# A fused attention and expert kernel: scale sizes, row gathers and weight measures put at other steps

## The chip, the cores and the metric

The kernel runs on one core of one Trainium2 chip. The metric is the device time of one execution in microseconds (us). Before the change it was 986.37 us, the median of three runs (983.27 to 987.94).

## The reference, cut to what matters

Eight batches of eight heads with 576 tokens of 64 features go through attention in which only scores within `tau` of the row's maximum count. The output is laid out as 4608 rows of 512 features. Each row then goes to one of eight experts:

```python
scores = scale * np.matmul(q, k.transpose(0, 1, 3, 2))
thresh = np.max(scores, axis=-1, keepdims=True) - tau
scores = np.where(scores >= thresh, scores, -1e9)
attn = softmax(scores)                       # with 1e-9 in the divisor
x = np.matmul(attn, v)                       # -> 4608 rows of 512
e_idx = np.argmax(x @ w_gate, axis=1)
out[mask_e] = gate_w * sigmoid(x @ w_output_gate)[e] * (relu(x @ w1[e]) @ w2[e])
```

The weights `w1[e]` are 512 x 1024 and `w2[e]` 1024 x 512, all in float32.

## The kernel before, in words

**Attention** (`Attention.run`, line 342) is a loop over columns `g`. Nine columns (`T`) are a step `m`, which takes two units (a unit is one head of a pair of batches), and there are 16 steps, so 144 columns (`G`, `end`), and six more that drain the pipeline. A column computes a tile of scores on PE (line 145), copies and reduces it on VectorE (159), takes exponentials on ScalarE (177) and masks on VectorE (189), transposes, and multiplies by v. The threshold between comes from GpSimd (166). The order in PE, VectorE, ScalarE and GpSimd is that of the program, written out by hand; SP's order, which issues the direct loads, is left to the framework's planner. Work from elsewhere is hung on columns by a table `hooks`, run at the column's end.

**Routing** (`Router`). After every fourth step a batch pair's rows are scattered by GpSimd (line 547) to `xs` in DRAM, grouped by expert. Rows of the first three pairs (group "A") fill the early units; the rest is spread over ten slots of fixed sizes, `SLOTS`. `choose` (679) picks greedily for each slot in turn which expert it serves; it is a generator, first one step and then three steps per slot (the third writes `picks`, line 701), and `aside` (497) runs some of its steps per column. `finish` (709) scatters rows of zeros behind the last row of each expert, the eight *pads*, and makes the remaining tables.

**Experts.** There are thirteen units: three early ones (366, 256 and 424 rows, units 0 to 2) and one per slot, in the order `UNITS` (780). `Experts.run` (1038) gives each unit eight columns `f`, each 128 of the 1024 hidden features: `first` (1178) multiplies rows by w1 (line 1187, 12 matmuls), ScalarE does the relu (1189), ScalarE and VectorE split the result into a high half `hh` and a low half `hl` (940, 946), and one column later `second` (1193) multiplies by w2 (1207 to 1209). Precision is kept by splitting each float32 operand in two float16 halves, after scaling by powers of two. So for the weights:

- `load_next` (1010) loads a chunk (a quarter of an expert, 1 MB in two DMAs, line 831) when a buffer is free and its slot is picked. There are four buffers for even and four for odd units.
- `look` (984) measures a chunk's largest value three columns later (`measure`, 855: VectorE line 858 and ScalarE line 859). In column 0 it measures whatever of the next unit is left, and `top` (866) reduces the eight numbers per row (869, 870: `red`), transposes them on PE (871) and takes the maximum. In column 3 `spread` (881) spreads it to all rows.
- `split_until` (1022) splits the chunks into halves (942 on ScalarE, 948 on VectorE).

And for the rows: `gather` loads them from `xs` into the one buffer `xg`, `even` (896) takes each row's largest value on VectorE (899, `ax`) and scales the row on ScalarE (906), `prep` transposes in two columns (1163, or 1279 for units whose size isn't whole tiles) and splits. Before the change the gather of unit i+1 is issued in column 0 of unit i (column 1 if that is unit 2), `even` in column 4 (5) and `prep` in columns 5 and 6 (6 and 7). `Pair.load` (1247) makes a slot's gather wait for all row scatters and all pads.

**During attention** the twelve chunks of the early units are loaded (`glance`) and measured (`size`) from hooks, one per nine columns, and after the last columns unit 0 is prepared by hooks.

Of the kernel before, what the change touches and what calls it, by code (L numbers as in the profile page):

```python
# [17 lines left out]
P = 128  # L18
# [412 lines left out]
class Router:  # L431
# [4 lines left out]
    def __init__(self, ctx, tc, ntok, E, DM, sizes, cut):  # L436
# [55 lines left out]
        self.odd = ctx.enter_context(tc.tile_pool(name="rodd", bufs=1))  # L492
        self.ripe, self.side, self.last = False, [], False
        self.xrows, self.queue, self.pending, self.placed, self.tables = {}, [], None, None, []
        self.gate, self.kind = None, None

    def aside(self, n):
        for _ in range(n):
# [210 lines left out]
    def finish(self):  # L709
        nc, E, sm, row, dummy = self.nc, self.E, self.sm, self.row, self.dummy  # L710
        V = nc.vector
        pad = sm.tile([P, E], F32, name="padf")
        padi = sm.tile([P, E], I32, name="padi")
        held = sm.tile([P, E], F32, name="held")
        V.tensor_scalar(pad, self.cnt, self.pid, None, op0=ALU.add)
        V.tensor_tensor(held, pad, self.first, op=ALU.subtract)
        V.tensor_scalar(held, held, float(self.SAFE), float(1 << 20), op0=ALU.is_lt, op1=ALU.mult)
        V.tensor_tensor(padi, pad, held, op=ALU.add)
        yield "vector"
        self.pads = []  # L720
        for e in range(E):
            self.pads.append(self.scatter(self.zrow, padi[:, e : e + 1], "pad"))
            if e % 2:
                yield "vector"
        while not self.chosen:
            yield "vector"
        ni, nf, v, ci, st = row(E, "ni", I32), row(E, "nf"), row(E, "v"), row(E + 1, "ci"), self.st
        V.tensor_scalar(nf, st[:, 0], float(P - 1), 0.0, op0=ALU.add, op1=ALU.max)
        V.tensor_copy(ni, nf)
        V.tensor_scalar(ni, ni, 7, None, op0=ALU.arith_shift_right)  # L730
        V.tensor_copy(nf, ni)
        V.tensor_scalar(v, st[:, 2], -1.0, dummy, op0=ALU.mult, op1=ALU.add)
        yield "vector"
        yield from self.sums(ci, nf)
        V.tensor_copy(self.total, ci[:, E : E + 1])
        yield from self.table(sm, "s", self.rows, ci, P, v)
        self.tables.append("s")
# [39 lines left out]

class Experts:
    RB, NW, YB = 4, 4, 4
    UNITS = (2, 6, 0, 7, 3, 8, 1, 5, 9, 4)  # L780
    TURN = (2,)
    LOOK, MEASURE = 3, 3

# [79 lines left out]
        V.tensor_scalar(up.bitcast(I32), src.bitcast(I32), EXPONENT, EXPONENT, op0=ALU.bitwise_and, op1=ALU.bitwise_xor)  # L863
        V.tensor_scalar(down.bitcast(I32), src.bitcast(I32), EXPONENT, None, op0=ALU.bitwise_and)

    def top(self, mx, ps):
        nc, V, n = self.nc, self.nc.vector, mx.shape[1]
        red = self.kp.tile([P, 8], F32, name="red")[:, 0:n]
        V.tensor_reduce(red, mx, axis=AX.X, op=ALU.max)
        V.tensor_scalar(red, red, UP, FLOOR, op0=ALU.mult, op1=ALU.max)  # L870
        nc.tensor.transpose(ps[0:n, 0:P], red, self.ident)

        def out():
            g = self.kp.tile([8, 1], F32, name="most")[0:n]
            self.diag = self.kp.tile([8, 8], BF16, name="diag")[0:n, 0:n]
            V.tensor_reduce(g, ps[0:n, 0:P], axis=AX.X, op=ALU.max)
            V.tensor_scalar(self.diag, self.ident[0:n, 0:n], g, None, op0=ALU.mult)

        return out
# [96 lines left out]
    def size(self, j):  # L976
# [3 lines left out]
        if e == 0:  # L980
            self.raws.append(raw)
            self.nload += 1

    def look(self, i, f, final):
        if self.fresh and self.column - self.fresh[0][2] >= self.LOOK:
            n, raw, _ = self.fresh.pop(0)
            if n % 4 == 0:
                self.mx[n // 4] = self.kp.tile([P, 2, 4], F32, name="mx")
            self.measure(raw, self.mx[n // 4], n % 4)
        n = i + 1  # L990
        if n < self.rt.early or final:
            return
        tile = lambda: self.ps_x.tile([P, 512], F32, name="px")
        if f == 0:
            while any(x[0] // 4 == n for x in self.fresh):
                k, raw, _ = self.fresh.pop(0)
                if k % 4 == 0:
                    self.mx[k // 4] = self.kp.tile([P, 2, 4], F32, name="mx")
                self.measure(raw, self.mx[k // 4], k % 4)
            self.top(self.mx.pop(n), tile())()  # L1000
        if f == 3:
            self.spread([n], tile())()

    def unit(self, i):
# [33 lines left out]
    def run(self):  # L1038
        rt, nun = self.rt, len(self.make)
        rt.open(self.ctx)  # L1040
        self.split_until(4)
        prev, fin = None, False
        for i in range(nun):
            b, final = self.unit(i), i == nun - 1
            late = i == rt.early - 1
            for f in range(8):
# [13 lines left out]
                    prev = (b, f)  # L1060
                self.look(i, f, final)
                k = f - (6 if late else 5)
                if not final and k == -1:
                    self.unit(i + 1).even()
                if not final and k in (0, 1):
                    self.unit(i + 1).prep(k)
# [4 lines left out]
                    rt.place(self.ps_x.tile([P, 512], F32, name="px")[:, 0:144])()  # L1071
                for _ in range(6 if rt.last else 3 if i or f else 0):
                    rt.advance(most=1)
                rt.aside(1 if rt.tables and i < rt.early else 2 if i else 4)
                if late and f == 1:
                    self.unit(i + 1).gather()
                self.split_until(2 * self.used + (4 if f % 2 else 3) - (i == 0))
                if final and f == 4:
                    self.tc.keep_in_program_order(self.nc.gpsimd.drain())
                if not (final or late) and f == 0:  # L1080
                    self.unit(i + 1).gather()
                self.load_next()
                self.column += 1
                if not rt.queue and not fin:
# [151 lines left out]
class Pair(Base):  # L1236
# [10 lines left out]
    def load(self, dst, r0, n):  # L1247
        rt = self.ex.rt
        src = rt.xs[bass.ds(self.row + r0, n), :]
        ins = self.nc.sync.dma_start(dst, src if n < P else src.rearrange("(t p) w -> p t w", p=P))  # L1250
        rt.after(ins, [x for _, x in rt.tok])
        rt.after(ins, rt.pads)

    def gather(self):
        self.xg = self.ex.gp.tile([P, 4, self.ex.rt.W], F32, name="xg")
# [149 lines left out]
def build(tc, qkv, tau, wg, w1, w2, out, shape):  # L1405
    nc = tc.nc
    with ExitStack() as ctx:
# [6 lines left out]
        with tc.manual_schedule(engines=ENGINES):  # L1414
            with ExitStack() as actx:
# [3 lines left out]
                end = at.G  # L1419
                ws = []  # L1420
                hooks[1] = lambda: ex.begin()
                W = 9
                for j in range(4 * rt.early):
                    g = end - 7 - W * (4 * rt.early - 1 - j)
                    hooks[g - 16] = lambda j=j: ex.glance(j)
                    hooks[g] = lambda j=j: ex.size(j)
                early = list(range(rt.early))
                hooks[end - 5] = lambda: at.jobs.append(lambda ps: ex.top(ex.early, ps))
                hooks[end - 3] = lambda: at.jobs.append(lambda ps: ex.spread(early, ps))
                hooks[end - 6] = lambda: ex.unit(0).gather()  # L1430
                hooks[end - 2] = lambda: outs.append(ex.unit(0).even(False))
                hooks[end - 1] = lambda: (ws.extend(ex.first_chunk()), outs.pop(0)())
                outs = []

                def prep(k):
                    pt = at.ps_s.tile([P, 1024], F32, name="ps")
                    ex.px = lambda: [pt[:, 0:512], pt[:, 512:]]
                    ex.unit(0).prep(k, outs)

                def second():  # L1440
                    prep(1)
                    outs[0]()
                    ws[0]()
                    ws[1]()

                def third():
                    outs[1]()
# [6 lines left out]
                    ws[2]()  # L1454
                    ws[3]()

                hooks[end] = lambda: prep(0)
                hooks[end + 1] = second
                hooks[end + 2] = third
                hooks[end + 4] = first  # L1460
                at.run(hooks)
            ex.open()
# [51 lines left out]
```

## Time and profile before

| | us |
|---|---|
| median of three runs | 986.37 |
| lowest and highest | 983.27, 987.94 |
| the profiled execution's own time | 986.73 |
| its span, first to last instruction | 985.0 |
| busy: PE, VectorE (DVE), ScalarE (ACT), GpSimd (POOL) | 899.8, 779.7, 734.0, 385.7 |

Times in the profile are us from the start of the span; `L871` is line 871 of the kernel before. Engines work side by side, so busy times don't add up to the span, and a matmul's end is modelled, so a busy PE isn't PE at its peak. What ends a wait is named behind an arrow. The granted clock is the share of TensorE's full clock of 2.4 GHz.

### The profile page before, as it was taken

To read this page: it belongs to the slowest core of one execution; us is meant where nothing else is said; L and a number is where in the kernel's file an instruction comes from. 1 tells how busy PE (TensorE), PEld (TensorE's weight loads), DVE (VectorE), ACT (ScalarE), POOL (GpSimd) and SP (SyncE) were. 2 spreads that over 40 slices of the span, in tenths; PEclk is the share of its full clock that TensorE was granted. 3 is DMA by queue.
4 is the path that set the end of the run, shared out by engine and by line. 5 is a ranking of instruction groups with operands and counts; after the bars stand their busy time and mean duration, and the time that the engine had idled before them with its cause. 6 is when DMAs were issued, how large, how long until landed. Compare 5 with 4: busy or idle time off the path is not lost. (4 is left out here: it accounts for less than half of the span.)

```text
span 985.0 us, 22613 instructions
## 1 busy us (share of the span) xinstructions
PE 899.8 (91%) x8367; PEld 544.0 (55%) x8367; DVE 779.7 (79%) x1889; ACT 734.0 (75%) x1406; POOL 385.7 (39%) x660
## 2 busy tenths in 40 slices
PE   8999999999999999999994596898898898898996
PEld 4666666665666666665553353445455345455543
DVE  7999999999999899999683756687677567668741
ACT  6999999998999989988762736567568567668642
POOL 4465657668666586776365000201002001002011
PEclk9999999999999999999898788899999999999999
DMA  4469633334433343331394605536545436544001
GB/s 158 144 220 293 179 122 98 107 110 138 133 121 109 118 152 96 111 115 55 114 325 158 201 22 178 200 99 201 171 150 163 150 109 190 171 150 141 22 21 43
DMA packets 77009, 136.92 MB, mean 139 GB/s; under 512 B 6792, under 2 KB 37768, under 8 KB 76897
## 3 DMA queue, kind: packets, MB, share of 16 engines
q1 hardware_dynamic: 70353, 115.29, 37.0%
q0 software_dynamic: 6544, 20.16, 5.4%
q8 instruction: 67, 1.10, 0.5%
q14 instruction: 45, 0.37, 0.1%
HBM read 103.65 MB, written 32.74 MB: 138 GB/s over the span
## 5 line engine op out<-in xcount | busy, mean ns | idle before, releaser
L177 ACT ACTIVATE p<-s,mn 128x576 f32<-128x576 f32 x288 | 215.3, 794 | 28.8 <-DVE s L159 28.6
L189 DVE SCALAR_TENSOR_TENSOR p<-s,thr,p 128x576 f32<-128x576 f32 x288 | 226.2, 822 | 5.0 <-POOL thr L166 4.4
L159 DVE TENSOR_SCALAR_CACHE_REDUCE s<-ps 128x576 f32<-128x576 f32 x288 | 206.2, 751 | 15.7 <-PE ps L145 13.9
L930 POOL DMA_INDIRECT out_dram<-yo,kid x39 | 46.3, 1186 | 382.6 <-DVE yo L929 244.6
L145 PE MATMUL ps<-qk 64*128 64x288 f32 (+1 forms) x1280 | 186.5, 419 | 0.7 <-DVE s L159 0.4
L166 POOL TENSOR_SCALAR thr<-mn,tau_sb 128x2 f32<-128x2 f32 x144 | 103.4, 718 | 134.2 <-DVE s L159 131.1
L1187 PE MATMUL ph<-xh,w1h 128*128 128x256 f16 (+7 forms) x412 | 135.9, 331 | 0.0
L1187 PE MATMUL ph<-xh,w1l 128*128 128x256 f16 (+7 forms) x412 | 134.8, 329 | 0.7 <-DVE w1l L948 0.7
L1187 PE MATMUL ph<-xl,w1h 128*128 128x256 f16 (+7 forms) x412 | 133.8, 329 | 0.0
L1189 ACT ACTIVATE hr<-ph 128x256 f32<-128x256 f32 (+7 forms) x103 | 48.0, 466 | 113.2 <-PE ph L1187 111.9
L145 PEld LDWEIGHTS ps<-qk 64*128 64x128 f32 (+1 forms) x1280 | 109.4, 177 | 21.8 <-DVE s L159 6.4
L946 DVE TENSOR_TENSOR hl<-hr,hh 128x256 f16<-128x256 f32 (+7 forms) x103 | 54.4, 528 | 78.3 <-ACT hh L940 75.4
L1187 PEld LDWEIGHTS <-w1h 128*128 128x128 f16 x832 | 81.8, 101 | 52.4 <-issue 6.2
L258 PE MATMUL pr<-PTb,vld 128*64 128x320 f32 (+1 forms) x640 | 107.1, 447 | 0.0
L244 PE MATMUL pt<-ident,p 64*128 64x64 f32 x2288 | 96.2, 224 | 1.5 <-ACT PTb L250 1.2
L244 PEld LDWEIGHTS pt<-ident,p 64*128 64x128 f32 x2288 | 83.4, 140 | 2.6 <-ACT PTb L250 1.5
L258 PE MATMUL pa<-PTa,vld 128*64 128x256 f32 (+1 forms) x640 | 84.7, 392 | 0.0
L1207 PE MATMUL py<-w2h,hh 128*128 128x512 f16 (+3 forms) x213 | 82.8, 389 | 0.0
L1208 PE MATMUL py<-w2l,hh 128*128 128x512 f16 (+3 forms) x213 | 82.7, 388 | 0.0
L1209 PE MATMUL py<-w2h,hl 128*128 128x512 f16 (+3 forms) x213 | 82.1, 385 | 0.5 <-DVE hl L946 0.2
L948 DVE SCALAR_TENSOR_TENSOR w1l<-r,up,w1h 128x1024 f16<-128x1024 f32 x40 | 51.2, 1280 | 30.0 <-ACT w1h L942 29.0
L324 POOL TENSOR_TENSOR rows<-xl,rinv 128x256 f32<-128x256 f32 x64 | 62.1, 970 | 14.6 <-ACT xl L369 14.3
(237 smaller groups left out, 1756.1 us busy)
## 6 DMA issues: line engine op xcount, KB each, us to landing
r<-in_moe_w_dram SPq DMA_DIRECT2D x120, 512.0 KB
qk<-in_qkv_dram SPq DMA_DIRECT2D x31, 608.0 KB
xs<-zrow SPq DMA_DIRECT2D x44, 257.0 KB
vld<-in_qkv_dram SPq DMA_DIRECT2D x32, 320.0 KB
xg<-xs SPq DMA_DIRECT2D x4, 771.0 KB
xg<-xs SPq DMA_DIRECT2D x6, 514.0 KB
xg<-xs SPq DMA_DIRECT2D x3, 1028.0 KB
xg<-xs SPq DMA_DIRECT2D x6, 128.5 KB
```

Source lines behind the costliest of these rows:

```text
L145: nc.tensor.matmul(ps[a][rows, o : o + HS], q[pp, t * P : t * P + w], k[pp, k0 : k0 + HS], start=True, stop=True)
L159: nc.vector.tensor_scalar(s, ps[a][:, c0 : c0 + S], SC, None, op0=ALU.mult, op1=ALU.min, accum_out=mn[:, a : a + 1])
L166: self.router.gate = nc.gpsimd.tensor_scalar(thr, mn, self.tau, None, op0=ALU.add)
L177: self.nc.scalar.activation(e, ss[a], AF.Exp, bias=mn[:, a : a + 1], scale=-1.0)
L189: nc.vector.scalar_tensor_tensor(e, s, thr[:, a : a + 1], e, op0=ALU.is_le, op1=ALU.mult, accum_out=acc[:, a ^ (t > 1) : (a ^ (t > 1)) + 1])
L244: nc.tensor.transpose(pt[:, o : o + 64], p[hs[h], k0 : k0 + P], id_[hs[h], hs[h]])
L258: one = lambda out, l, r, start, stop: nc.tensor.matmul(out, l, r, start=start, stop=stop, skip_group_check=True)
L324: nc.gpsimd.tensor_tensor(o, xl[:, a, 0:4, 0:D], ra[:, a, 0:4, None].broadcast_to([P, 4, D]), op=ALU.mult)
L1187: nc.tensor.matmul(ph, w[:, c, fs], x[:, c, 0:N], start=(i == 0), stop=(i == 11))
L1207: nc.tensor.matmul(Y, hh[:, ts], wh, start=(f == 0), stop=False)
L1208: nc.tensor.matmul(Y, hh[:, ts], wl, start=False, stop=False)
L1209: nc.tensor.matmul(Y, hl[:, ts], wh, start=False, stop=(f == 7))
```

## The change

- **Measures in other steps of attention.** The twelve chunks are measured in steps 2, 3, 4, 6, 7, 8, 10 to 15 (third column), instead of steps 4 to 15, and loaded in a list of columns instead of sixteen columns ahead.
- **Unit 0's start.** Its gather moves from column `end - 6` to `end - 2`, its pass over the rows from `end - 2` to `end`, behind the first weight half; transposes, key and second half follow one column later each.
- **Sizes.** `top` is cut in two: `peak` makes `red` in column 0, the transposition comes in column 3 and `spread` in column 4.
- **Rows.** `even` comes in column 3 (4 in unit 2). The gather of unit i+2 comes in column 7 of unit i, if it is an early unit or a picked slot with all pads issued; unit 3 keeps its place in unit 2.
- **Unit 3** takes slot 0 (420 rows) and unit 5 slot 2 (512 rows). A gather from slot 0 doesn't wait for the pads.
- **Picking.** Two steps per column in unit 2, where it was one.

```diff
-        self.gate, self.kind = None, None
+        self.gate, self.kind, self.pads = None, None, []
...
-    UNITS = (2, 6, 0, 7, 3, 8, 1, 5, 9, 4)
+    UNITS = (0, 6, 2, 7, 3, 8, 1, 5, 9, 4)
...
-    def top(self, mx, ps):
-        nc, V, n = self.nc, self.nc.vector, mx.shape[1]
+    def peak(self, mx):
+        V, n = self.nc.vector, mx.shape[1]
         red = self.kp.tile([P, 8], F32, name="red")[:, 0:n]
         V.tensor_reduce(red, mx, axis=AX.X, op=ALU.max)
         V.tensor_scalar(red, red, UP, FLOOR, op0=ALU.mult, op1=ALU.max)
+        return red
+
+    def top(self, red, ps):
+        nc, V, n = self.nc, self.nc.vector, red.shape[1]
         nc.tensor.transpose(ps[0:n, 0:P], red, self.ident)
...
+    def settled(self, i):
+        rt = self.rt
+        return i < rt.early or i > rt.early and self.known(i) and len(rt.pads) == rt.E
...
         if f == 0:
             while any(x[0] // 4 == n for x in self.fresh):
...
-            self.top(self.mx.pop(n), tile())()
+                self.weigh()
+            self.most = self.peak(self.mx.pop(n))
         if f == 3:
+            self.top(self.most, tile())()
+        if f == 4:
             self.spread([n], tile())()
...
-                if not final and k == -1:
+                if not final and k == -2:
                     self.unit(i + 1).even()
...
-                rt.aside(1 if rt.tables and i < rt.early else 2 if i else 4)
+                rt.aside(1 if rt.tables and i < 2 else 2 if i else 4)
                 if late and f == 1:
                     self.unit(i + 1).gather()
+                    self.gathered = i + 1
...
-                if not (final or late) and f == 0:
+                if not (final or late) and f == 0 and self.gathered < i + 1:
                     self.unit(i + 1).gather()
+                    self.gathered = i + 1
+                if f == 7 and i + 2 < nun and self.settled(i + 2):
+                    self.unit(i + 2).gather()
+                    self.gathered = i + 2
...
-        rt.after(ins, rt.pads)
+        if self.s == 0:
+            rt.tc.declare_no_dep(ins.ins, group="pad", reason="rows of their own")
+        else:
+            rt.after(ins, rt.pads)
...
-                W = 9
-                for j in range(4 * rt.early):
-                    g = end - 7 - W * (4 * rt.early - 1 - j)
-                    hooks[g - 16] = lambda j=j: ex.glance(j)
-                    hooks[g] = lambda j=j: ex.size(j)
+                size = (2, 3, 4, 6, 7, 8, 10, 11, 12, 13, 14, 15)
+                load = (0, 4), (1, 4), (2, 4), (4, 4), (5, 4), (6, 4), (8, 4), (9, 4), (10, 0), (10, 6), (12, 4), (13, 4)
+                for j, (m, s) in enumerate(load):
+                    hooks[at.T * m + s] = lambda j=j: ex.glance(j)
+                    hooks[at.T * size[j] + 2] = lambda j=j: ex.size(j)
...
-                hooks[end - 6] = lambda: ex.unit(0).gather()
-                hooks[end - 2] = lambda: outs.append(ex.unit(0).even(False))
-                hooks[end - 1] = lambda: (ws.extend(ex.first_chunk()), outs.pop(0)())
+                hooks[end - 2] = lambda: ex.unit(0).gather()
+                hooks[end - 1] = lambda: ws.extend(ex.first_chunk())
...
+                def begin():
+                    ws[0]()
+                    ex.unit(0).even()
+                    ws[1]()
+
                 def second():
                     prep(1)
                     outs[0]()
-                    ws[0]()
-                    ws[1]()
...
-                hooks[end] = lambda: prep(0)
-                hooks[end + 1] = second
-                hooks[end + 2] = third
+                hooks[end] = begin
+                hooks[end + 1] = lambda: prep(0)
+                hooks[end + 2] = second
+                hooks[end + 3] = third
                 hooks[end + 4] = first
```

## Rows read from the trace of the kernel before

**Rows 1.** The page's second part: PE's busy tenths in 40 slices of the span.
```profile
PE   8999999999999999999994596898898898898996
```

**Rows 2.** Windows of attention steps 2, 4, 5: length, each engine's busy time, clock, DMA.
```profile
core 0: us, PE busy (x) PEld busy (x) DVE busy (x) ACT busy (x) POOL busy (x), PEclk, DMA share, GB/s
59.50:87.50 28.00, 28.00 (x364) 18.35 (x366) 26.39 (x75) 25.62 (x55) 16.80 (x26) 1.00 0.85 262
115.40:143.40 28.00, 28.00 (x364) 18.32 (x366) 27.44 (x76) 26.54 (x57) 16.92 (x27) 1.00 0.35 115
143.40:173.00 29.60, 29.40 (x366) 18.86 (x368) 29.29 (x85) 27.34 (x59) 19.00 (x40) 1.00 0.32 104
```

**Rows 3.** Timeline of VectorE in steps 3 and 4: start, length, instruction, idle before.
```profile
97.49 0.76 DVE L159 TENSOR_SCALAR_CACHE_REDUCE s<-ps 128x576 f32<-128x576 f32 x1 [1.19 <-PE ps L145]
...
124.19 1.16 DVE L858 TENSOR_REDUCE early<-r 128x1 f32<-128x1024 f32 x1
```

**Rows 4.** Waits of PE over the span: total us, times, longest.
```profile
PE px L871 <- DVE red L870: 34.5, 10, 11.8
PE px L1279 <- ACT xg L906: 25.6, 9, 18.6
```

**Rows 5.** Timeline of PE, three waits: end of attention, (2, 0), (5, 0).
```profile
469.17 0.33 PE L212 MATMUL pa<-ident,p 64*128 64x64 f32 x1 [2.06 <-DVE p L189]
...
566.46 0.37 PE L871 MATMUL px<-ident,red 128*2 128x128 f32 x1 [4.80 <-DVE red L870]
...
697.32 0.27 PE L871 MATMUL px<-ident,red 128*2 128x128 f32 x1 [2.67 <-DVE red L870]
```

**Rows 6.** Windows behind three stalls of PE (columns as in rows 2).
```profile
566.50:571.70 5.20, 5.20 (x16) 2.31 (x17) 1.90 (x6) 0.56 (x2) 2.23 (x2) 0.51 0.27 101
...
618.20:622.20 4.00, 4.00 (x11) 1.42 (x12) 2.59 (x10) 0.45 (x1) 0.00 (x0) 0.50 1.03 362
...
697.50:701.00 3.50, 3.50 (x13) 1.58 (x12) 1.68 (x3) 0.00 (x0) 1.20 (x3) 0.56 0.76 282
```

**Rows 7.** Waits of SP's queue: total us, times, longest.
```profile
SPq L1331 <- DMA xs<-zrow,padi: 13.1, 1, 13.1
```

**Rows 8.** Timeline of SP, 524 to 605 us.
```profile
524.13 0.40 SPq L831 DMA_DIRECT2D r<-in_moe_w_dram  x1
537.73 1.57 SPq L1331 DMA_DIRECT2D xg<-xs  x3
...
601.54 3.32 SPq L831 DMA_DIRECT2D r<-in_moe_w_dram  x5
```

**Rows 9.** Timeline of POOL: the fourth and the eighth pad.
```profile
523.45 1.77 POOL L547 DMA_INDIRECT xs<-zrow,padi  x1 [0.30 <-issue]
...
533.88 0.97 POOL L547 DMA_INDIRECT xs<-zrow,padi  x1 [0.30 <-issue]
```

**Rows 10.** Timeline of VectorE: unit 0's pass, unit 2's columns, unit 4's pass.
```profile
464.12 1.69 DVE L899 TENSOR_REDUCE ax<-xg 128x3 f32<-128x1536 f32 x1
...
585.70 0.60 DVE L946 TENSOR_TENSOR hl<-hr,hh 128x424 f16<-128x424 f32 x1 [1.52 <-ACT hh L940]
...
590.00 0.60 DVE L946 TENSOR_TENSOR hl<-hr,hh 128x424 f16<-128x424 f32 x1 [1.83 <-ACT hh L940]
...
599.96 0.13 DVE L701 TENSOR_SCALAR picks<-got 1x1 int32<-1x1 f32 x1
...
677.63 2.28 DVE L899 TENSOR_REDUCE ax<-xg 128x4 f32<-128x2048 f32 x1
```

**Rows 11.** Timeline of ACT in unit 4 (256 rows).
```profile
672.70 0.36 ACT L1189 ACTIVATE hr<-ph 128x256 f32<-128x256 f32 x1
...
675.30 0.38 ACT L1189 ACTIVATE hr<-ph 128x256 f32<-128x256 f32 x1 [0.76 <-PE ph L1187]
...
680.40 2.56 ACT L906 ACTIVATE xg<-xg,xup 128x512 f32<-128x512 f32 x4 [2.67 <-issue]
...
683.90 0.36 ACT L1189 ACTIVATE hr<-ph 128x256 f32<-128x256 f32 x1
```

More of the change, by code (lines that the diff above doesn't have):

```diff
@@ L719, in finish @@
         yield "vector"
-        self.pads = []
         for e in range(E):
@@ L982, in size, with weigh @@
             self.nload += 1
+    def settled(self, i):
+        rt = self.rt
+        return i < rt.early or i > rt.early and self.known(i) and len(rt.pads) == rt.E
+    def weigh(self):
+        n, raw, _ = self.fresh.pop(0)
+        if n % 4 == 0:
+            self.mx[n // 4] = self.kp.tile([P, 2, 4], F32, name="mx")
+        self.measure(raw, self.mx[n // 4], n % 4)
     def look(self, i, f, final):
         if self.fresh and self.column - self.fresh[0][2] >= self.LOOK:
[L986 to L989, printed above, removed]
+            self.weigh()
         n = i + 1
@@ L995, in look @@
             while any(x[0] // 4 == n for x in self.fresh):
[L996 to L999, printed above, removed]
-            self.top(self.mx.pop(n), tile())()
+                self.weigh()
+            self.most = self.peak(self.mx.pop(n))
         if f == 3:
+            self.top(self.most, tile())()
+        if f == 4:
             self.spread([n], tile())()
@@ L1041, in run @@
         self.split_until(4)
-        prev, fin = None, False
+        prev, fin, self.gathered = None, False, 0
         for i in range(nun):
@@ L1421, in build @@
                 hooks[1] = lambda: ex.begin()
-                W = 9
-                for j in range(4 * rt.early):
-                    g = end - 7 - W * (4 * rt.early - 1 - j)
-                    hooks[g - 16] = lambda j=j: ex.glance(j)
-                    hooks[g] = lambda j=j: ex.size(j)
+                size = (2, 3, 4, 6, 7, 8, 10, 11, 12, 13, 14, 15)
[3 more added lines that the diff above has]
+                    hooks[at.T * size[j] + 2] = lambda j=j: ex.size(j)
                 early = list(range(rt.early))
-                hooks[end - 5] = lambda: at.jobs.append(lambda ps: ex.top(ex.early, ps))
+                hooks[end - 5] = lambda: at.jobs.append(lambda ps: ex.top(ex.peak(ex.early), ps))
                 hooks[end - 3] = lambda: at.jobs.append(lambda ps: ex.spread(early, ps))
-                hooks[end - 6] = lambda: ex.unit(0).gather()
-                hooks[end - 2] = lambda: outs.append(ex.unit(0).even(False))
-                hooks[end - 1] = lambda: (ws.extend(ex.first_chunk()), outs.pop(0)())
+                hooks[end - 2] = lambda: ex.unit(0).gather()
+                hooks[end - 1] = lambda: ws.extend(ex.first_chunk())
                 outs = []
```

## The prediction, made before the result was known

> **What bounds the kernel now.** I read the slices of the page first [rows 1]. PE shows 9 for twenty-two slices and drops to 4 or 5 three times near 530, 565 and 610 us; afterwards it never holds 9 for long. PE's "busy" hides who leads while attention runs, so I cut attention into its steps of nine columns [rows 2]. A step without routing work lasts 28.0 us, one with it (steps 5 and 9) 29.6, and there VectorE is busy 29.29 of 29.60: VectorE sets the pace of attention. In steps 1 to 3 it idles once per step, 1.19 us, waiting for a score tile [rows 3]; in step 4 a weight measure of 1.16 us sits in exactly that place and the step is still 28.0 long.
>
> From column 144 on the question is where PE stands. The waits of PE [rows 4] give two groups: 34.5 us in ten waits for `red`, the maximum from which a unit's weight scale is made, and 25.6 us for scaled rows `xg` in nine, 18.6 of it in one wait. The ten are 4.80 us once [rows 5], 11.8 once, and eight that share the remaining 17.9, of which 2.67 us at 697.32 is typical. Windows behind three of these stalls [rows 6] show the second price: 5.2, 4.0 and 3.5 us of matmuls at a granted clock of 0.51, 0.50 and 0.56, so at 1.2 GHz instead of 2.4, after PE had stood still. Half of such a stretch is lost: 2.6, 2.0 and 1.75 us.
>
> Why the two big stalls: SP waited 13.1 us for pad scatters [rows 7], so the gather of unit 2 went out at 537.73 although SP had nothing before it since 524.13 [rows 8]; and the last pad left POOL only at 534.85, though the fourth had left at 525.22 [rows 9]. The stall near 606 starts with a pick of a slot: VectorE wrote it at 599.96 [rows 10], SP began that unit's weights at 601.54 [rows 8], and the size could not be taken before they had landed.
>
> **The change, part by part.** I write (unit, column).
>
> *Measures in other steps.* The measures of steps 5 and 9 go to steps 2 and 3, where the 1.19 us idle takes one each [rows 3]. Steps 5 and 9 lose 1.16 each: **-2.3**. Their 24 loads leave SP up to two steps sooner and stand ahead of the q, k, v loads. These run two units ahead, a whole step of 28 us, so I cost it at nothing; without that cover a chunk of 1.05 MB at 362 GB/s [rows 6] is 2.9 us, three of them at most +9, to be kept in mind for the high end.
>
> *The end of attention.* Unit 0's pass over its rows (1.69 us [rows 10] and three short instructions, about 2.1) leaves the last attention columns, where PE waited 2.06 us for the masks behind it [rows 5], and is done a step later with the first weight half ahead of it; transposes, key and the second half each slide one step. The gather only waits for scatters, so its hook on SP costs nothing. The gain lies between -5 (the wait and the slow clock behind it) and +3.1 (a column, 28.0 / 9, by which the transposes slide). Nearest is the wait itself, on the same columns: **-3** with a little of the clock.
>
> *Unit 2's gather at (0, 7) instead of (1, 0).* Four pads are issued up to then, three output scatters and four pads after. Its reads overlap what a pad may write, so it still waits for those ahead of it: POOL's fourth instead of eighth pad, 534.85 - 525.22 = 9.6 us sooner. But VectorE's pass, moved one column forward too, now holds up (1, 4)'s low half and PE has that second product, 1.3 us or 2.6 at half clock, still to do; ScalarE's copies and the weights' high half stand before it. I take half of 9.6 for the stall and 3 more from measures of unit 3, whose weights come sooner since slot 0 is the first pick: **-7.5**. Bounds: 0 (SP holds the weights behind the gather instead), -18.6 (no wait at all).
>
> *Unit 3.* It takes slot 0, known two picks sooner, and waits for no pads. Its four chunks are then measured before (2, 0), and the transpose of `red` comes three columns after its making. The stall of 4.80 and its slow stretch go, 4.8 + 2.6: **-7.4**. If its weights were late, 0.
>
> *Two picking steps per column in unit 2 instead of one.* Slot 6, unit 4's, is complete with the 22nd step (one, then three per slot), which was at (2, 6). Now it is done at (2, 3), three columns of 4.3 us (`hl` at 585.70 and 590.00) [rows 10], 13 us sooner, and four chunks need 11.6 us at 362 GB/s [rows 6]. The weights then land by (2, 6), the size is transposed at (3, 3). The stall of 11.8 and 2.0 of clock go: **-13.8**. Bounds 0 and that. An extra step is three or four instructions like the one of 0.13 us at 599.96, with gaps some 0.6 to 0.7 us of VectorE a column; it is idle before `hl` in those columns (the waits behind `hh`) [rows 10], so they cost nothing; uncovered, seven columns times 0.7 = +5.
>
> *Sizes in units 4 to 11.* The eight waits of 17.9 us were PE at column 0 standing behind VectorE's output scaling, a measure and the reduction. PE now goes on with two products. Behind a small unit (256 rows) comes a large one whose columns cover that backlog; behind a large one comes a small one and the backlog returns as a late `hl`. I take three quarters, 13, and the slow stretches after the three small-to-large waits, 3 x 1.75 = 5.2: **-18**. Bounds: -9 (half, no clock) and -24.
>
> *The pass over rows a column earlier, all units.* What ends last here is told by ScalarE's rows [rows 11] with the pass [rows 10]. In unit 4, `ax` starts at 677.63, the four copies at 680.40, and the relu of the next column runs only at 683.90, behind them and a weight half, 6.3 us after `ax`; a column is 2.6 (relus at 672.70 and 675.30). The copies' wait is what PE sees today, 2.6 us. Moved one column, that wait for `xg` goes, but the relu one column earlier now stands behind the copies. PE has queued some 3.9 us (first, second, first) against 6.3 plus 0.8 for cast and low half, so it waits 3.2 or more at a second product, and what it did before the stall (1.3) is left for after. Against 2.6 that is about 1.5 to 2 worse in each of units 4, 6, 8 and 11, which are small with four tiles to follow: **+6**. Bounds: -10 (2.6 gone in all four), +10 (a whole column more). Large units have columns of 4.3 or more and cover it.
>
> Here a rule speaks against this step. The Trainium skill, "PSUM — Partial Sum Buffer", section "Engine vs sequencer instructions", says ScalarE's and VectorE's queues are strict FIFO. By it every instruction behind a waiting copy waits as well, and the sum has +6. Judged by the `xg` waits [rows 4] alone, as if a relu could pass, it would have -10 and the time would be 924. The relu at 683.90 [rows 11] agrees with the rule.
>
> *The rest.* Gathers in column 7 stand on SP ahead of that column's weights. Unit i+1's rows are last read by transposes in column 6, so SP isn't held long; each takes 0.4 to 1.6 us to issue [rows 8], hidden as SP mostly waits. POOL's order changes nowhere. The tail of the last unit is untouched.
>
> Sum: -2.3 - 3 - 7.5 - 7.4 - 13.8 - 18 + 6 = -46. The profiled execution took 986.7 us (985.0 span, 1.7 around it), 0.4 above the median, so 986.7 - 46 = **940.7**; I say 940, a little of the 0.4 included.
>
> **The rivals.** *Stalls move more than they go* (25%). The gather of unit 2 is issued earlier but holds SP with unit 3's weights behind it; the first stall stays (+7.5), the second halves (+3.7), the small units lose a full column (+4): 940 + 15 = 955, up to 968 if the column 0 sizes give half only. For it: VectorE and ScalarE have little room in small units, and both serve in order. Against: slot 0 is picked two picks sooner, which lets SP have the weights first.
>
> *More goes* (14%). The gather of unit 2 finds nothing to wait for: the first stall shrinks by 11 more, and the earlier passes cost nothing (-6): 923, or 913 if their waits go too. For: 18.6 is the largest stall; against: the wait that names the pads [rows 7].
>
> *Slower: SP held at gathers* (4%). In column 7 a gather that waits for its buffer holds the next unit's weights, their measures come late, and the wait for `red` returns as it was before unit 4, 11.8 + 2.0 = 13.8 a unit, now at the next product. It decides from the fourth unit of nine on (46 / 13.8 = 3.3); with five, 940 + 69 = 1009. For: SP is one queue and waits a lot; against: the buffer is free one column before.
>
> *It doesn't do what it says* (3%): picks, pads and passes all turn out covered by VectorE's load, and only step moves of 2 to 4 us are left: 984, no change.
>
> **How the numbers follow.** The forecast, 54%, spans 926 to 950. I let the range reach from 915, which takes in most of the case with more gain, to 963, which takes in most of the moved stalls: about 2 in 10 stay out. What this kernel can tell from no change is about 0.5%, 5 us. Faster 0.54 + 0.25 + 0.14 = 0.93; same 0.03; slower 0.04.
>
> **What would show it.** Steps 5 and 9 near 28.4 us, 2 and 3 still 28.0. No PE wait on `red` above 0.5 us. The first big stall between 8 and 16 us, ended by the low half and not by `xg`; none near 606. SP's gather of unit 2 some 3 us after the fourth pad has left POOL, and before the eighth. In units 4, 6 and 8 a PE wait of 3 to 5 us for `hl` in column 4 or 5. I am wrong if the waits for `red` come back under another name at equal length, or if PE stays idle 18 us at unit 2.

## The result, and the profile after

The changed kernel takes 942.58 us, the median of four runs (941.37 to 944.89); the kernel before took 984.82 (982.47 to 987.94) beside it. The ratio is 0.957, with a 95% interval from 0.954 to 0.961. The profiled execution took 943.19 us, its span is 941.5. Line numbers are from here on those of the changed kernel: relu 1203, casts to high halves 943, low halves 949, weights' high halves 945, pass over the rows 902, row copies 909, measures 857 and 858, second products 1221 to 1223 (1317 to 1319 in transposed units), weight loads 830.

The first part of the page after: VectorE, ScalarE and GpSimd are busy as long as before within 3 us; PE 12 us less, as less of its work ran at half clock (its mean granted clock rose from 0.960 to 0.972), and 31 us of its idle time went (985.0 - 899.8 before, 941.5 - 887.4 after).

```profile
PE 887.4 (94%) x8367; PEld 538.2 (57%) x8367; DVE 779.5 (83%) x1889; ACT 731.6 (78%) x1406; POOL 385.5 (41%) x660
```

The second part, PE's slices, to be held against [rows 1]. Of three deep dips one is left.

```profile
PE   8999999999999999999999398898998998999896
```

PE's longest waits after the change (total us, times, longest), where [rows 4] had 34.5 us for `red` and 25.6 for `xg`, and two of them in PE's timeline.

```profile
PE py L1221 <- ACT hh L943: 31.7, 6, 14.2
PE py L1318 <- DVE hl L949: 3.3, 3, 2.0
PE py L1317 <- ACT hh L943: 2.2, 2, 1.3
```
```profile
535.34 0.61 PE L1221 MATMUL py<-w2h,hh 128*128 128x512 f16 x1 [14.18 <-ACT hh L943]
...
647.57 0.61 PE L1221 MATMUL py<-w2h,hh 128*128 128x512 f16 x1 [4.05 <-ACT hh L943]
```

Of both old names hardly anything is left: 0.4 us for `red`, at the end of attention, and 1.5 for `xg`, in unit 0. What is left waits for `hh`, the cast behind a relu: once 14.18 us in unit 1, and in the units 4, 6, 8, 10 and 11 (256 rows each) 4.05, 4.10, 4.09, 1.77 and 3.48.

Where the 43.5 us of span went is read from marks in ScalarE's timeline, the first relu of a unit or column, before and after; for attention from VectorE's first score copy of each step.

| stretch, and its mark | before, after | gain so far | this stretch | predicted |
|---|---|---|---|---|
| attention, start of step 15 | 437.3, 430.1 | -7.2 | -7.2 | -2.3 |
| end of attention, (0, 0) | 482.83, 474.86 | -8.0 | -0.8 | -3 |
| unit 1 and its stall, (2, 0) | 560.40, 548.23 | -12.2 | -4.2 | -7.5 |
| second stall, (2, 1) | 571.11, 551.67 | -19.4 | -7.3 | -7.4 |
| rest of unit 2, (3, 0) | 604.28, 586.50 | -17.8 | +1.7 | 0 |
| third stall, (3, 1) | 623.35, 591.80 | -31.6 | -13.8 | -13.8 |
| rest of unit 3, (4, 0) | 661.05, 627.64 | -33.4 | -1.9; for equal rows +4.6 | 0 |
| units 4 to 11, (12, 0) | 937.64, 894.21 | -43.4 | -10.0; for equal rows -16.5 | -18 + 6 |

"For equal rows": unit 3 has 420 rows instead of 512 now and unit 5 the reverse. A unit in which PE never waits takes 39.95 us with 512 rows and 33.50 with 420 (unit 5 after the change, and in the run with the old order of slots, below), so some 6.45 us only changed places.

### The profile page after: what moved, and what is told of

Its sections match the earlier page's. It is cut to its first block, busy times and chain, and to the rows that moved or that the text cites. A ratio compares the mean times of both kernels' runs of the same rounds, so it can differ in the third digit from the quotient of the medians.

```text
span 941.5 us, 22582 instructions
## 1 busy us (share of the span) xinstructions
PE 887.4 (94%) x8367; PEld 538.2 (57%) x8367; DVE 779.5 (83%) x1889; ACT 731.6 (78%) x1406; POOL 385.5 (41%) x660
## 5 line engine op out<-in xcount | busy, mean ns | idle before, releaser
L933 POOL DMA_INDIRECT out_dram<-yo,kid x39 | 44.3, 1135 | 356.5 <-DVE yo L932 222.1
L166 POOL TENSOR_SCALAR thr<-mn,tau_sb 128x2 f32<-128x2 f32 x144 | 101.5, 705 | 131.6 <-DVE s L159 127.4
L1201 PE MATMUL ph<-xh,w1h 128*128 128x256 f16 (+7 forms) x412 | 131.5, 320 | 0.0
L1201 PE MATMUL ph<-xh,w1l 128*128 128x256 f16 (+7 forms) x412 | 130.6, 319 | 0.7 <-DVE w1l L951 0.7
L1201 PE MATMUL ph<-xl,w1h 128*128 128x256 f16 (+7 forms) x412 | 129.6, 319 | 0.8 <-DVE xl L949 0.8
L951 DVE SCALAR_TENSOR_TENSOR w2l<-r,up,w2h 128x1024 f16<-128x1024 f32 x40 | 51.3, 1282 | 33.5 <-ACT w2h L945 32.4
```

The costliest lines, as they stand in the source:

```text
L166: self.router.gate = nc.gpsimd.tensor_scalar(thr, mn, self.tau, None, op0=ALU.add)
L1201: nc.tensor.matmul(ph, w[:, c, fs], x[:, c, 0:N], start=(i == 0), stop=(i == 11))
```

## Experiments

Each is the changed kernel with the edit shown, or with several of them where the text says so; the kernel before ran beside every group at 986.0 to 986.5 us. Ratios are to it; the changed kernel's is 0.957.

### Attention: which steps hold loads and measures

```diff
-                load = (0, 4), (1, 4), (2, 4), (4, 4), (5, 4), (6, 4), (8, 4), (9, 4), (10, 0), (10, 6), (12, 4), (13, 4)
+                load = (0, 4), (1, 4), (2, 4), (4, 4), (5, 4), (7, 4), (8, 4), (9, 4), (10, 0), (11, 4), (12, 4), (13, 4)
```

> The changed kernel with two of the twelve weight chunks loaded in steps 7 and 11 (fifth column) again, as before the change, instead of steps 6 and 10; they are measured in the same columns as in the changed kernel. In the traces steps 7 and 11 became 1.9 and 2.8 us shorter, and a copy of GpSimd that waited 1.8 and 3.3 us for row scatters no longer does. Theory: a chunk's 1 MB shares the DMA engines with the scatters of these steps, these land later and GpSimd, then VectorE wait: 4 to 5 us slower, about 947 us, with both waits back. Rival: the two steps became shorter because of other work moved (measures, phase of the routing): no change, 942 to 943.

Measured: 944.94 us (943.25 to 948.33), ratio 0.959 [0.956, 0.961]. Steps 7 and 11 took 30.62 and 32.48 instead of 29.28 and 29.73, 4.1 us more together. In the total only 2.4 of the expected 4 to 5 us show, which alone would not be clear of noise (the intervals overlap): step 15 begins 4.8 us later, but the units 4 to 11 came out 3.1 us shorter in the profiled run, with unchanged code. So the reading rests on the two steps. The second edit puts all twelve loads and measures back where they were.

```diff
-                size = (2, 3, 4, 6, 7, 8, 10, 11, 12, 13, 14, 15)
-                load = (0, 4), (1, 4), (2, 4), (4, 4), (5, 4), (6, 4), (8, 4), (9, 4), (10, 0), (10, 6), (12, 4), (13, 4)
-                for j, (m, s) in enumerate(load):
-                    hooks[at.T * m + s] = lambda j=j: ex.glance(j)
-                    hooks[at.T * size[j] + 2] = lambda j=j: ex.size(j)
+                W = 9
+                for j in range(4 * rt.early):
+                    g = end - 7 - W * (4 * rt.early - 1 - j)
+                    hooks[g - 16] = lambda j=j: ex.glance(j)
+                    hooks[g] = lambda j=j: ex.size(j)
```

> The twelve loads and measures of attention go back to their old columns; everything else as in the changed kernel. Theory (the new columns are worth 7.2 us: 1.6 for the measures in the scatter steps 5 and 9, the rest for weight chunks that no longer run beside row scatters in steps 3, 7 and 11): step 15 begins 6.5 to 7.5 us later and the total is 948 to 951; VectorE's waits for GpSimd's threshold are back at 3 to 5 us. Rival (my prediction: only the measures cost, 2.3): step 15 begins 2 to 3 us later, total 944.5 to 946.

Measured: 948.39 us (946.64 to 949.78), 0.962 [0.959, 0.964]; step 15 begins at 437.2 instead of 430.1, 7.1 later. The waits between 140 and 460 us show why, first in the changed kernel, then in the one with one pair of loads moved, then with all of it back.

```profile
POOL sums L196 <- DMA xs<-rows,dsti: 0.5, 1, 0.5
DVE p L189 <- POOL thr L166: 0.2, 1, 0.2
```
```profile
POOL sums L196 <- DMA xs<-rows,dsti: 4.6, 2, 3.3
DVE p L189 <- POOL thr L166: 4.1, 4, 2.8
```
```profile
POOL sums L196 <- DMA xs<-rows,dsti: 5.7, 3, 2.7
DVE p L189 <- POOL thr L166: 4.5, 4, 2.4
```

In the kernel before one of these places reads as follows: SP's, GpSimd's and VectorE's timelines in step 7.

```profile
217.00 0.93 SPq L831 DMA_DIRECT2D r<-in_moe_w_dram  x2
```
```profile
225.77 0.18 POOL L196 COPY sums<-acc 64x1 f32<-64x1 f32 x1 [1.80 <-DMA xs<-rows,dsti]
226.22 0.29 POOL L166 TENSOR_SCALAR thr<-mn,tau_sb 128x2 f32<-128x2 f32 x1 [0.27 <-POOL sums L196]
```
```profile
226.55 1.17 DVE L189 SCALAR_TENSOR_TENSOR p<-s,thr,p 128x576 f32<-128x576 f32 x1 [1.49 <-POOL thr L166]
```

A weight chunk goes out while rows are being scattered; the scatters end later, GpSimd's small copy waits for them, the threshold stands behind that copy, and VectorE, which sets the pace, waits for the threshold. The windows of steps 5, 7 and 11 after the change, without that meeting:

```profile
143.40:172.20 28.80, 28.80 (x366) 19.02 (x368) 28.46 (x82) 26.27 (x57) 18.95 (x40) 1.00 0.34 107
200.30:229.60 29.30, 29.30 (x370) 19.27 (x370) 28.91 (x81) 27.18 (x57) 20.17 (x32) 1.00 0.29 95
314.40:344.10 29.70, 29.70 (x368) 19.31 (x370) 29.27 (x79) 27.15 (x57) 20.25 (x32) 1.00 0.29 95
```

Steps 5 and 9 gained 0.8 each (29.60 before [rows 2]), steps 7 and 11 1.9 and 2.8, step 14 0.9: 7.2. The last 0.9 isn't the change's: with the same attention step 14 took 28.9 us in four profiled runs and 29.9 in six.

### The end of attention

Unit 0's hooks go back to their old columns.

```diff
-                hooks[end - 2] = lambda: ex.unit(0).gather()
-                hooks[end - 1] = lambda: ws.extend(ex.first_chunk())
+                hooks[end - 6] = lambda: ex.unit(0).gather()
+                hooks[end - 2] = lambda: outs.append(ex.unit(0).even(False))
+                hooks[end - 1] = lambda: (ws.extend(ex.first_chunk()), outs.pop(0)())
...
-                hooks[end] = begin
-                hooks[end + 1] = lambda: prep(0)
-                hooks[end + 2] = second
-                hooks[end + 3] = third
+                hooks[end] = lambda: prep(0)
+                hooks[end + 1] = second
+                hooks[end + 2] = third
```

> Unit 0's gather, pass, transposes, key and second weight half go back to the columns of the kernel before; everything else as in the changed kernel. Theory (most of what I had booked for the tail never was there: the first relu comes 8.0 us sooner after the change and 7.2 of it is already there when step 15 begins): the first relu moves later by 0.5 to 2 us, total 943 to 945. Rival (the tail is worth the 3 us that I predicted, and attention less): 3 or more later, 945.5 to 948.

Measured: 944.14 us (942.39 to 945.14), 0.957 [0.954, 0.960]. PE's 2.06 us wait for the masks [rows 5] is back in full, and yet from step 15 to the first relu it is 45.6 us against 44.8: the edit seems worth 0.8 us. One profile doesn't settle so little, since two other runs with the new hooks took 45.6 and 45.7 there. But from the start of step 14 to the first relu the twelve profiled runs with the new hooks took 73.6 to 74.7 us and the two with the old ones 75.3 and 75.6, so about 1 us is likely. In the old order the transposes come a column sooner, which is the likely reason that the wait's going bought so little; that was not tried by itself. The total is 1.6 us longer; 1.9 us of lag was there when step 15 began, and that is no part of the edit.

### Unit 2's gather, and what stands behind it

With the column 7 gather left out, unit 2's gather goes out in column 0 of unit 1 behind all eight pads.

```diff
-                if f == 7 and i + 2 < nun and self.settled(i + 2):
-                    self.unit(i + 2).gather()
-                    self.gathered = i + 2
```

> The changed kernel with the gathers in column 0 of the unit before again instead of column 7 two units ahead. Theory: only unit 2's gather matters; it waits for eight pads instead of four and lands 6 to 10 us later, VectorE's early pass holds up PE so much longer: 6 to 12 us slower, about 951, and nothing changes in units 3 to 12, whose rows land in time. Rival: in the other units too rows land late for the pass in column 3, and PE waits there: more than 14 us slower.

Measured: 950.90 us, 0.964 [0.962, 0.967]. SP's and PE's timelines:

```profile
530.53 1.58 SPq L1345 DMA_DIRECT2D xg<-xs  x3
532.36 12.80 SPq L830 DMA_DIRECT2D r<-in_moe_w_dram  x2
```
```profile
544.20 0.61 PE L1218 MATMUL py<-w2h,hh 128*128 128x512 f16 x1 [22.88 <-ACT hh L943]
```

The stall is 8.7 us longer, which is all of the loss; the units behind are not slower (so the gathers of the other units in column 7 are worth nothing). Then the opposite: unit 2's gather waits for no pad at all. Its rows lie behind all experts' regions in `xs`, where no pad goes.

```diff
         rt.after(ins, [x for g, x in rt.tok if g == "A"])
+        rt.tc.declare_no_dep(ins.ins, group="pad", reason="rows of their own")
```

> The changed kernel with the gather of unit 2 declared free of the pads, whose rows it does not read. Theory: what is left of the first big stall, 14.2 us of PE, is the wait for the fourth pad; without it the gather goes out 8 to 12 us sooner, the stall shrinks to 3 to 6 us and the kernel takes 931 to 935 us. Rival: the scaled rows are late because SP and the DMA engines are busy with weights, or the stall is VectorE's backlog: 0 to 3 us faster only.

Measured: 934.54 us, 0.947 [0.945, 0.949]: 8.0 us, as the theory said, though 6.77 us of the stall are left. SP, ScalarE and PE in this run:

```profile
505.82 1.97 SPq L1348 DMA_DIRECT2D xg<-xs  x3
508.05 21.19 SPq L830 DMA_DIRECT2D r<-in_moe_w_dram  x6
```
```profile
521.50 1.06 ACT L858 ACTIVATE junk<-r 128x1024 bf16<-128x1024 f32 x1 [5.04 <-DMA r<-in_moe_w_dram]
```
```profile
528.28 0.61 PE L1221 MATMUL py<-w2h,hh 128*128 128x512 f16 x1 [6.77 <-ACT hh L943]
```

And the same place in the changed kernel: GpSimd's fourth pad [rows 9], SP's wait for it [rows 7], SP [rows 8], VectorE's pass, ScalarE.

```profile
516.97 1.77 POOL L547 DMA_INDIRECT xs<-zrow,padi  x1 [0.30 <-issue]
```
```profile
SPq L1348 <- DMA xs<-zrow,padi: 12.2, 1, 12.2
```
```profile
521.12 1.61 SPq L1348 DMA_DIRECT2D xg<-xs  x3
522.98 13.32 SPq L830 DMA_DIRECT2D r<-in_moe_w_dram  x5
```
```profile
528.21 2.29 DVE L902 TENSOR_REDUCE ax<-xg 128x4 f32<-128x2048 f32 x1 [9.19 <-DMA xg<-xs]
```
```profile
529.38 1.06 ACT L858 ACTIVATE junk<-r 128x1024 bf16<-128x1024 f32 x1 [13.35 <-DMA r<-in_moe_w_dram]
```

The gather went out 2.4 us behind the fourth pad, as predicted. But it stood between the two halves of unit 3's second chunk (nineteen half chunks of the units 1 to 3 ahead of it, five behind), and ScalarE's measure of the second half, first in its queue, waited 13.35 us for it; the relu for (1, 4) stands behind that. So two things hold the stall, the rows on VectorE and the weights on ScalarE, and both stood on SP's queue behind one wait of 12.2 us.

### The pass over the rows a column earlier

```diff
-                if not final and k == -2:
+                if not final and k == -1:
                     self.unit(i + 1).even()
```

> The changed kernel with the pass over the rows (even) put back one column later, all else as changed. In the changed kernel PE waits 31.7 us in six waits for the high half of a relu that stands behind the scaling copies. Theory of the in-order queues: the pass a column earlier costs about 1.5 us in each of units 4, 6, 8 and 11, so this kernel is 4 to 8 us faster than the changed one, about 936 us, and its waits in small units are for scaled rows (2.0 to 2.6 us each). Rival: the earlier pass is what lets the transposes run without a wait, so this kernel is 6 to 12 us slower, about 952.

Measured: 934.48 us (934.34 to 939.90), 0.949 [0.946, 0.951]. With the pass late again PE's waits are 9.79 and 3.25 us in unit 1 (14.18 in one before the edit: nothing won by (2, 0)) and 2.22, 2.25, 2.85, 1.14 and 1.26 in the five small units, 9.7 in place of 17.5. PE's longest waits in this run:

```profile
PE px L1177 <- ACT xg L909: 10.2, 14, 2.2
PE py L1221 <- ACT hh L943: 9.8, 1, 9.8
PE px L1296 <- ACT xg L909: 7.4, 7, 3.3
```

ScalarE's timeline of unit 4 in the changed kernel, to be read beside [rows 11]:

```profile
643.22 2.56 ACT L909 ACTIVATE xg<-xg,xup 128x512 f32<-128x512 f32 x4 [4.06 <-DVE xdown L863]
645.68 1.13 ACT L945 ACTIVATE w2h<-r,up 128x1024 f16<-128x1024 f32 x1
646.72 0.36 ACT L1203 ACTIVATE hr<-ph 128x256 f32<-128x256 f32 x1
```

The relu stands behind four copies and a weight half, and PE goes on 0.85 us after it (647.57). The Trainium skill, "PSUM — Partial Sum Buffer", section "Engine vs sequencer instructions", calls ScalarE's and VectorE's queues strict FIFO. The trace agrees: copies from 643.22, weight half at 645.68, relu at 646.72, one behind the other. So of +6 and -10 the first was the right side to take: from (2, 0) to (12, 0) the late pass is 7.1 us shorter.

Both edits at once:

> The changed kernel with both edits that were faster by themselves: the pass over the rows a column later, and unit 2's gather free of the pads. Theory: they act at different places (small units; the stall at unit 2) and add up: 934.5 - 8 = about 926 to 928 us. The later pass also let PE do one more product before unit 2's stall, so a part may be counted twice. Rival: both gains come from unit 2's stall alone: about 932 to 934.

Measured: 933.88 us (929.75 to 935.49), 0.945 [0.943, 0.948]. They don't add, and the time is the rival's. In unit 1 the late pass now costs, since the pass is no longer held up by its rows: PE waits twice, 4.14 and 3.26 us, in place of once, 6.77, and unit 2 starts 3.7 us later than with the free gather alone (543.94 against 540.28). But the rival's reason doesn't hold, since the run after this one is 4.8 us shorter behind unit 2's start than the free gather alone. In this profile, the slowest of the five runs, only a part of it shows: from (2, 0) to (12, 0) it is 342.5 us, against 345.1 with the free gather alone and 338.9 with the late pass alone. So the pass was put early in unit 1 alone, with the free gather kept:

```diff
-                if not final and k == -2:
+                if not final and k == (-2 if i == 1 else -1):
```

> Unit 2's gather doesn't wait for the pads, and the pass over the rows stays in its new, earlier column in unit 1 alone; in all other units it goes back a column. Theory (early is good where nothing else holds the pass up and a long stall stands behind it, and costs 6 or 7 us in the units behind): the 8.0 of the free gather and 3.5 to 7 of the later pass add up, 928 to 931. Rival (the gain of the later pass lies in unit 1 or in the granted clock, not in the small units): 933 to 936.

Measured: 929.77 us (928.27 to 931.64), 0.943 [0.940, 0.946]; unit 2 starts at 540.04, as with the free gather alone, and from there to (12, 0) it is 340.3 us against 346.0 in the changed kernel.

### Sizes, picks and slots

The transposition of `red` goes back to column 0 and the spreading to column 3.

```diff
             self.most = self.peak(self.mx.pop(n))
+            self.top(self.most, tile())()
         if f == 3:
-            self.top(self.most, tile())()
-        if f == 4:
             self.spread([n], tile())()
```

> The changed kernel with the sizes transposed in column 0 again, right behind VectorE's reduction, and spread in column 3. Theory: the eight waits for red in units 4 to 11 come back with 13 to 18 us and the slow clock behind them, and so does one at unit 3 and one at unit 4 (2 to 5 each): 15 to 22 us slower than the changed kernel, about 961 us. Rival: the backlog of VectorE returns anyway as late low halves, the transposes three columns later only move it: 5 us or less, about 946.

Measured: 968.62 us, 0.982 [0.980, 0.984]. It is the largest single part: 26 us, more than the 22 that the theory allowed, and the wait of [rows 4] is back beside the new ones (PE's waits in this run).

```profile
PE py L1220 <- ACT hh L943: 32.2, 6, 14.7
PE px L874 <- DVE red L869: 23.2, 10, 4.0
```

By the marks 20.3 us of it lie in the units 4 to 11 and 5.4 between (3, 0) and (3, 1). Then one picking step per column in unit 2:

```diff
-                rt.aside(1 if rt.tables and i < 2 else 2 if i else 4)
+                rt.aside(1 if rt.tables and i < 3 else 2 if i else 4)
```

> The changed kernel with one picking step per column in unit 2 again. Theory: unit 4's slot is picked three columns later, its weights start 13 us later, VectorE waits in unit 3's first column for data that it must measure there, and with it everything in order behind it: 9 to 14 us slower than the changed kernel, about 954 us, with a stall near unit 3's column 0 or 1. Rival: the three columns between measure and transposition absorb most of it, and VectorE has less to do in unit 2: 0 to 4 us slower.

Measured: 950.55 us, 0.963 [0.960, 0.966]: 8 us, between theory and rival. Unit 4's chunks land one by one in front of ScalarE, and PE waits as it did before the change, but half as long, since the later transposition already covers the rest:

```profile
599.22 1.06 ACT L858 ACTIVATE junk<-r 128x1024 bf16<-128x1024 f32 x1 [1.70 <-DMA r<-in_moe_w_dram]
```
```profile
602.43 0.51 PE L1317 MATMUL py<-hh,w2h 128*128 128x420 f16 x1 [5.89 <-ACT hh L943]
```

Last the slots in their old order, unit 3 waiting for all pads.

```diff
-    UNITS = (0, 6, 2, 7, 3, 8, 1, 5, 9, 4)
+    UNITS = (2, 6, 0, 7, 3, 8, 1, 5, 9, 4)
...
-        if self.s == 0:
-            rt.tc.declare_no_dep(ins.ins, group="pad", reason="rows of their own")
-        else:
-            rt.after(ins, rt.pads)
+        rt.after(ins, rt.pads)
```

> The changed kernel with slot 2 (512 rows) as unit 3 and slot 0 (420 rows) as unit 5 again, unit 3's gather waiting for all pads. Theory: unit 3's weights wait for the third pick instead of the first, they come after unit 2's gather and are measured late: a stall of 3 to 7 us before unit 3's weights are split, and 3 to 8 us slower in all, about 948. Rival: unit 3 with 512 rows gives PE 7 us more to do while VectorE makes the tables, where the changed kernel loses 5 to 6 us; so the order costs nothing, or this kernel is faster, 936 to 942.

Measured: 938.89 us (937.29 to 940.49), 0.952 [0.949, 0.955], so 3.7 faster, as the rival said. Windows of units 3 and 5 in this run, then in the changed kernel, and VectorE in the first 24 us of unit 3 there:

```profile
588.51:632.01 43.50, 42.90 (x227) 20.95 (x226) 36.28 (x74) 28.77 (x45) 5.62 (x5) 1.00 0.38 129
...
662.89:696.39 33.50, 33.50 (x206) 18.82 (x205) 24.61 (x36) 23.69 (x38) 2.94 (x3) 1.00 0.52 173
```
```profile
586.50:627.64 41.14, 36.91 (x228) 21.16 (x227) 35.52 (x75) 27.39 (x45) 5.53 (x5) 1.00 0.43 137
...
661.21:701.16 39.95, 39.95 (x205) 18.80 (x204) 24.75 (x35) 25.11 (x38) 2.71 (x3) 1.00 0.43 141
```
```profile
586.00:610.00 24.00, 21.24 (x124) 12.29 (x124) 23.02 (x57) 13.74 (x23) 5.53 (x5) 1.00 0.42 134
```

In unit 3 VectorE also does the routing's last table arithmetic (lines 727 to 774), and 23.02 of 24 us are taken. With 512 rows PE is busy nearly all of its 43.50 us; with 420 it idles 4.2 of 41.14. That the tables are what holds PE there is read from these windows; no run moved them. The second stall does not return (unit 2's first two relus are 3.96 us apart): the later transposition is enough, slot 0 was not needed. With slot 0 and the sizes at once 1.55 us of the 4.80 are left.

The three that helped, together: the free gather, the pass early in unit 1 alone, the old order of slots.

> As the run before, and the slots in their old order, so that unit 3 has 512 rows and unit 5 has 420. Theory (unit 3 is held by VectorE's table work, which longer columns of PE cover): 3 to 4 us below the run before, 924 to 928. Rival (the 3.7 us of the old order were unit 5's small-to-large step or the clock, and go when the pass is later): equal to the run before within 1.5.

Measured: 925.45 us (921.92 to 932.37), 0.939 [0.935, 0.942], the fastest version here by its median, 1.8% below the changed kernel; its interval still touches that of the run before. Two of its six runs took 932 and four 922 to 926.5. The profiled one, 932.37, has a wait that no other profile has (ScalarE's waits):

```profile
ACT hr L1203 <- remote: 11.5, 2, 7.5
```

Both times are relus in unit 1, and what they waited for the trace does not say; that stays open.

## Why the prediction was right, and where its terms were off

The time was 943 against 940, and the direction held for the reasons given: the waits for `red` and `xg` went, and the gather left behind the fourth pad and before the eighth. The closeness of the total is partly luck, since misses of 2 to 5 us in single terms nearly cancel. Term by term:

- **Measures, -2.3: mis-sized, -7.2 (some 6.3 of it the change's).** I priced the measures alone and costed the moved loads at nothing. The measures gave 0.8 a step instead of 1.16. The larger part was the loads: with them back in the scatter steps, 4.1 of 4.7 us returned. I followed the moved loads along SP's queue and did not ask what GpSimd's scatters meet in those steps.
- **The tail, -3: mis-sized, about -0.8.** PE's wait of 2.06 us did go, but the transposes slid by a column, the opposite bound of that term, and by that took most of it back, as far as the order tells.
- **First stall, -7.5: mis-sized, -4.2.** The lower bound's mechanism, weights behind the gather on SP, was at work: ScalarE stood 13.35 us at a measure. The run without pads shows 8 us more were to be had, less than the 11 of the rival that had more go; ScalarE then still stood 5.04 us at a measure, so the weights became the later of the two.
- **Second stall, -7.4: right in size, wrong in part of its reason.** The column 3 transposition is enough; slot 0 alone would have left 1.55 us.
- **Third stall, -13.8: right.** Twice the picking is worth 8 of it; without the later transposition 5.4 come back.
- **Sizes, -18: somewhat small.** Put back they cost 20.3 in the units 4 to 11; from the table, -16.5 less the pass's 5.7 there is -22. I had taken three quarters of the waits; nearly all went.
- **The pass, +6: right,** 7 to 8 measured, where and how it was said: a wait of 3.2 us or more at a second product (4.05). Only its name was off: `hh`, since already the relu is late, and not `hl`. The bound of -10 was read too wide: before the change PE waited for scaled rows 2.62, 2.00, 2.62 and 0.88 us in the units 4, 6, 8 and 11, and not 2.6 in each (a part of these waits stands at line 1163 and not in [rows 4]).
- **Not foreseen: unit 3, +4.6.** With 420 rows for 512 I moved the unit's matmuls and not what they cover. That VectorE has the tables to make there was in the code, and I looked only at the picks. The run with the old order gives 4.1 of the 4.6 back (43.50 against 41.14 + 6.45).

The misses nearly cancel: attention 4.9 better and the sizes some 4, the tail, first stall and unit 3 about 10 worse, the rest of unit 2 1.7. Of that last one 0.9 is the second picking step, which I had costed at nothing: with one step per column it is 34.0 us from (2, 1) to (3, 0) instead of 34.8.

Some figures of the prediction don't come out as written, and nothing hangs on them: in [rows 1] PE's nines before the first dip are twenty slices, and the third dip goes to 6 only; half of 9.6 and 3 is 7.8 and not 7.5; 955 and the 9 us by which half the gain of the sizes is less make 964 and not 968.

## What to carry to other kernels

When something is pulled forward, list what stands behind it on each in-order queue before counting its gain: here the pass held up relus, and a gather held up half a weight chunk. A producing pass should be early only where nothing else is waiting in that column, so decide it per unit. Keep large loads out of the stretches in which another engine waits for its own small scatters.

## What the runs showed of the hardware

- A 1 MB weight load near a group of row scatters made GpSimd wait up to 3.3 us for those scatters, with the DMA engines 0.35 to 0.40 busy on average over these steps. How the two meet inside the DMA engines no run shows.
- Equal waits do not cost the same in clock. Behind the same wait of 2.21 or 2.22 us in unit 4, with short waits for the next copies behind it, TensorE's granted clock over the next 4 us was 0.72 in the run with the late pass, 0.62 with the free gather besides and 0.83 with the pass early in unit 1 (windows, one each):

```profile
646.90:650.90 4.00, 2.99 (x23) 2.05 (x24) 1.16 (x1) 3.97 (x8) 0.00 (x0) 0.72 0.01 2
```
```profile
642.50:646.50 4.00, 3.05 (x23) 2.10 (x24) 1.11 (x1) 3.97 (x8) 0.00 (x0) 0.62 0.01 2
```
```profile
638.20:642.20 4.00, 2.98 (x26) 2.10 (x27) 1.14 (x1) 3.97 (x8) 0.00 (x0) 0.83 0.01 2
```

These are means over stretches at 2.4 and at 1.2 GHz. Unit 4 took 32.01, 33.26 and 32.14 us in them, with the same code for the unit, so about 1 us per small unit is chance, and gains of a few us should not be read from one profile.
